# A preamble scheduled by hand and fenced, with two weights converted in it, and weight loads moved to ScalarE's queue

## The chip, the core and the metric

The kernel runs on one core of a Trainium2 chip. Times are microseconds on the device, taken as the median of three runs. Beside them stands one profiled execution with its trace. PE is TensorE (PEld its weight loads), DVE is VectorE, ACT is ScalarE, POOL is GpSimd, and SP is SyncE, which issues transfers and computes nothing.

## The reference

Three stages follow each other. The first is windowed attention over 4 batches, 8 heads, 768 positions and 64 dimensions: each query sees the keys within 16 positions and one summary per block of 32 keys.

```
k_sum = k.reshape(B, H, nb, 32, D).max(axis=3);  v_sum = v.reshape(B, H, nb, 32, D).mean(axis=3)
scores = concat([where(|i - j| < 16, scale * q @ k.T, -1e9), scale * q @ k_sum.T + log(32)])
a = softmax(scores);  x = a @ concat([v, v_sum])            # 3072 tokens x 512
h = x @ w_in;  x = (h * cos(h)) @ w_out                     # 512 -> 2048 -> 512
logits = x @ phi;  d = softmax(logits, over tokens);  slots = d.T @ x      # 8 experts, 4 slots each
out = softmax(logits, over slots) @ (relu(slots @ w1) @ w2)
```

The weights `w_in` and `w_out` arrive as 64-bit numbers, whose two 32-bit halves the kernel turns into one f32 itself.

## The kernel before, in words

The middle stage is the long one. Its tokens are cut into 6 blocks of 512 and the 2048 hidden columns into 16 slices of 128, so that a loop of 96 slots runs block by block over the slices. In slot s PE computes `mm1`, 12 products of 128x512 into `h` (L384, L385, L388), DVE and ACT compute h cos h, and PE multiplies the result by `w_out` two slots later in `mm2`, again 12 products (L425, L426, L429). Every f32 operand is split into a high part that ACT casts (`wih`, `woh`, `gh`, `xh`) and a low part that DVE or POOL subtracts (`wil`, `wol`, `gl`, `xl`), which gives the three products where one would do.

Attention is cut into 24 groups of 4 heads by 4 query blocks. Groups 0 to 3 make the first token block and come in a preamble ahead of the loop. Groups 4 to 23 are worked off between the slots: scores on PE, exponentials on ACT, normalisation, transposes (`tr`, copied to `aT`), and the product with the values (`av`), which is split into `xh` and `xl`.

Each of the 16 weight slices is used by all six blocks and converted once. `load_w` (L119) brings 1 MB `raw` into one of two buffers. `conv_1` reads it twice on ACT (L129 and L130), `conv_2` shifts on DVE (L136), and `conv_3` adds on POOL (L141). Before, the string `PRE` (L44) lists the preamble token by token. It holds the conversions of slices 0 to 3 (`c0` to `c3`), and slice f from 4 on is converted in slot f - 4, whose load is for slice f + 2. The preamble's scores (`first_A`, L236) add the mask on PE, by two products with a split mask (L252), and the exponentials (`first_exps`, L261) read PSUM. The sums of the values, `vs`, are copied by ACT into the last rows of the value tiles (L225).

All instructions before slot 17 are put in an order by a scheduler that simulates the program; from slot 17 on (`MAN0`) PE and SP keep the order of the code. Each engine runs its instructions in order, and SP issues all transfers in one order too. `HB` (L53) sets in half slots where groups 4, 5 and 6, 7 begin; a negative value begins at slot 0. `fill` (L565) issues products of ones with ones that nothing reads.

Of the kernel before, what the change touches and what calls it, by code (L numbers as in the profile page):

```python
# [52 lines left out]
HB = (-4, 14)  # L53
# [25 lines left out]
def body(ctx: ExitStack, tc: tile.TileContext, q0, qk, kT, vn, vx, w, phi, ex, cst, out):  # L79
# [16 lines left out]
    NM = 6 * KC  # L96
    mask = att.tile([128, 6, KC], F32, name="mask", tag="mask", bufs=1)
# [18 lines left out]
    def load_w(f):  # L116
        pool, tag, n = (xres, "xl", 2) if f == 2 else (m2, ("x2", "x2T")[(f - (f > 2)) % 2], 1)
# [3 lines left out]
    def conv_1(f):  # L121

        W[f] = wres.tile([128, 2, 512], F32, name=f"w{f}", tag=f"w{f}")
        pool, tag = (wres, "w15") if f % 2 and f < 15 else (att, "cv")
# [1 line left out]
        nc.scalar.activation(W[f], raw[f][:, :, :, 1].bitcast(F32), AF.Prelu, scale=2.0 ** -111, alpha=-2.0 ** 32)  # L129
# [106 lines left out]
    def first_A(g, j):  # L236

        d = grp[g]
        ps = d["ps", j] = bank(f"sc{g}_{j}")
        c = (g // 2) % 3  # L240
        heads = [slice(64 * hh, 64 * hh + 64) for hh in range(2)]
        p = 2 * (g % 2) + j
        for u in range(4):
            o = QB * (4 * (g // 2) + u)
            for r in heads:
                nc.tensor.matmul(ps[r, u * KC:u * KC + KL], d["q"][r, j, u, :], kfirst[p][r, o:o + KL],
                                 start=u == 0, stop=False)
            for r in heads:
                nc.tensor.matmul(ps[r, u * KC + KL:(u + 1) * KC], d["q"][r, j, u, :], ksums[p][r, :],
                                 start=False, stop=False)  # L250
        for m in (mask_hi, mask_lo):
            nc.tensor.matmul(ps[:, 0:4 * KC], ident8, m[:, c:c + 4, :].rearrange("p w c -> p (w c)"),  # L252
                             start=False, stop=m is mask_lo)
        if j == 0:
            d["mx"] = stat.tile([128, 8], F32, name=f"mx{g}", tag="mx")
        m = d["mx"][:, 4 * j:4 * j + 4]
        nc.vector.tensor_reduce(out=m, in_=ps[:, 0:4 * KC].rearrange("p (w c) -> p w c", c=KC), axis=AX.X,
                                op=ALU.max, negate=True)
        nc.vector.tensor_single_scalar(out=m, in_=m, scalar=SCALE, op=ALU.mult)

    def first_exps(g, j):  # L261
        d = grp[g]
        if j == 0:
            if g % 2 == 0:
                grp["S", g // 2] = att.tile([128, 16, KC], F32, name=f"S{g}", tag="S")
            d["S"] = grp["S", g // 2][:, 8 * (g % 2):8 * (g % 2) + 8, :]
            d["sm"] = stat.tile([128, 8], F32, name=f"sm{g}", tag="sm")
        for u in range(4 * j, 4 * j + 4):
            c = (u % 4) * KC
            nc.scalar.activation(d["S"][:, u, :], d["ps", j][:, c:c + KC], AF.Exp, bias=d["mx"][:, u:u + 1],  # L270
                                 scale=SCALE, accum_out=d["sm"][:, u:u + 1])

    def att_A(g):
# [6 lines left out]
        pss = [ps_m.tile([128, 512], F32, name=f"sc{g}_{hh}", tag="m") for hh in range(2)]  # L280
        for n in range(4):
            for u in (2 * (n % 2), 2 * (n % 2) + 1):
                for hh in range(2):
                    t = d["qk"][64 * hh:64 * hh + 64, n // 2, u, :]
                    o = 64 * (u % 2)
                    nc.tensor.matmul(pss[hh][o:o + 64, n * KC:(n + 1) * KC], t[:, 0:QB], t[:, QB:], start=True, stop=True)  # L286
# [45 lines left out]
    def att_C(g, j):  # L332
# [9 lines left out]
        nc.scalar.copy(aT, ps[:KC, :])  # L342
        d["aT", j] = aT

    def att_D(g):
        d = grp[g]
        ps = bank(f"av{g}") if g < 4 else ps_m.tile([128, 512], F32, name=f"av{g}", tag="m")
        for j in range(2):
            for u in range(4):
                c = 256 * j + QB * u  # L350
                for hh in range(2):
                    r = slice(64 * hh, 64 * hh + 64)
                    a = d["aT", j][:, 128 * u + 64 * hh:] if g < 4 else d["aT", hh][:, 256 * j + 64 * u:]
                    nc.tensor.matmul(ps[r, c:c + QB], d["v"][:KC, j, u, r], a[:, 0:QB], start=True, stop=True)  # L354
# [207 lines left out]

# [12 lines left out]
    def masks():
        nc.vector.tensor_single_scalar(out=ident8, in_=ident, scalar=8.0, op=ALU.mult)
        nc.scalar.copy(mask_hi, mask)
        nc.gpsimd.tensor_tensor(out=mask_lo, in0=mask, in1=mask_hi, op=ALU.subtract)

    def load_mask2(_):  # L580

        nonlocal mask2
        mask2 = att.tile([128, 6, KC], F32, name="mask2", tag="mask", bufs=1)
        nc.sync.dma_start(out=mask2[:, 0:4, :].rearrange("p w c -> p (w c)"), in_=cst[:, NM + 468:NM + 468 + 4 * KC])

    mask2 = None

    C = lambda t, o, n: (lambda _: nc.sync.dma_start(out=t, in_=cst[:, o:o + n]))
    todo = dict(F=lambda _: fill(F0), f=lambda _: fill(NFILL), I=C(ident, NM, 128), M=C(mask.rearrange("p w c -> p (w c)"), 0, NM),
                A=C(avg, NM + 128, 52), S=C(sel, NM + 180, 288), N=load_mask2, P=lambda _: nc.sync.dma_start(out=phis.rearrange("p k s -> p (k s)"), in_=phi),  # L590
                K=load_kraw, Q=load_q_first, W=load_w, B=lambda i: load_vb(0, i), V=load_v, G=load_qk, X=load_vs,
                m=lambda _: masks(), k=ksum, s=scores, e=exps, v=lambda _: vsum_first(), t=turn, d=att_D, c=convert, c1=conv_1,
                w=lambda f: split_w(f, 0), a=att_K)
    for token in PRE.split():
        n = token.lstrip("FfIMNASPKQWBVGXmksevtdcwa")
        todo[token[:len(token) - len(n)]](int(n or 0))
# [347 lines left out]
```

## Time and profile before

| | us |
|---|---|
| median of 3 runs | 783.22 (782.16 to 784.07) |
| profiled execution | 780.9 |
| its span, first to last instruction | 778.9 |
| PE busy in the span | 740.2 (95%) |
| DVE, ACT, POOL busy | 473.6, 433.4, 428.6 |

The profiled execution is 2.3 us below the median, and 2.0 us of it lie outside the span. PE is the busy engine over the whole, but the shares differ by stretch: `fill` products count as busy, and in the first 120 us PE waits at several places. The granted TensorE clock is given as a share of 2.4 GHz; over the span it is 0.987.

### The profile page before, as it was taken

The numbers are of one execution on the slowest core, as the hardware profiler recorded it, in microseconds if no ns is written. First come the engines' busy times: TensorE is split into PE (matmuls) and PEld (weight loads), VectorE is DVE, ScalarE is ACT, GpSimd is POOL, SyncE is SP. The second block draws the span as 40 slices with busy tenths as digits, with TensorE's granted clock in tenths as the row PEclk, the third lists the DMA queues.
The fourth block names the chain that finished last, engine by engine and source line by source line (L and its number), as shares of the span: only waits on it lengthen the run. The fifth ranks groups of instructions, "written<-read, shape, count | busy, mean of one in ns | idle before, by whom it ended". The sixth has DMA issues, their size and how long they took to land.

```text
span 778.9 us, 13853 instructions
## 1 busy us (share of the span) xinstructions
PE 740.2 (95%) x5517; PEld 573.5 (74%) x5517; DVE 473.6 (61%) x686; ACT 433.4 (56%) x786; POOL 428.6 (55%) x302
## 2 busy tenths in 40 slices
PE   9977799998999999998999999999999999999994
PEld 7866678776877787776787777778768888786453
DVE  4578896767477576576575684774773444433523
ACT  4979868636465455574465555464554455443222
POOL 2555884365557657556566566665576665752000
PEclk9997999999999999999999999999999999999998
DMA  9988753121120331311211211301101922328978
GB/s 331 396 264 331 271 164 113 42 97 59 48 95 1 100 105 29 121 68 41 87 44 33 72 40 33 111 0 35 33 1 56 392 93 82 109 81 299 371 306 268
DMA packets 35585, 101.69 MB, mean 131 GB/s; under 512 B 3393, under 2 KB 13889, under 8 KB 33473
## 3 DMA queue, kind: packets, MB, share of 16 engines
q1 hardware_dynamic: 35520, 100.81, 36.8%
q8 instruction: 43, 0.70, 0.4%
q14 instruction: 22, 0.17, 0.1%
HBM read 92.54 MB, written 6.29 MB: 127 GB/s over the span
## 4 chain that ended last, share of the span: by engine, by line
PE 63%; DVE 13%; ACT 12%; DMA 6%; issue 4%; SPq 0%; ACTq 0%; DVEq 0%
PE acc L425 8%; PE h L384 8%; PE acc L426 8%; PE h L385 8%; PE acc L429 7%; PE h L388 7%; PE av L354 3%; DVE S L329 2%; DMA qk<-in_qk_dram 2%; PE yp L842 2%; DMA kr<-in_kT_dram 2%; PE sc L286 2%; PE hp L809 2%; ACT a L404 2%; DVE a L403 2%
## 5 line engine op out<-in xcount | busy, mean ns | idle before, releaser
L373 POOL TENSOR_TENSOR wol<-w,woh 128x512 fp32r<-128x512 f32 x96 | 143.9, 1500 | 115.0 <-ACT woh L372 115.0
L413 POOL TENSOR_TENSOR gl<-a,gh 128x512 fp32r<-128x512 f32 x96 | 129.0, 1343 | 83.8 <-ACT gh L412 78.3
L384 PE MATMUL h<-xh,wih 128*128 128x512 f32 x384 | 156.4, 407 | 6.7 <-DVE a L409 6.6
L425 PE MATMUL acc<-woh,gh 128*128 128x512 f32 x384 | 157.4, 410 | 3.5 <-DVE x L448 3.5
L385 PE MATMUL h<-xl,wih 128*128 128x512 f32 x384 | 152.2, 396 | 0.0
L426 PE MATMUL acc<-wol,gh 128*128 128x512 f32 x384 | 152.1, 397 | 0.0
L373 POOL TENSOR_TENSOR wil<-w,wih 128x512 fp32r<-128x512 f32 x81 | 113.9, 1406 | 42.8 <-PE h L388 24.2
L402 DVE TENSOR_SCALAR a<-h 128x512 f32<-128x512 f32 x96 | 65.9, 686 | 115.8 <-PE h L388 110.7
L404 ACT ACTIVATE a<-a,halfpi 128x512 f32<-128x512 f32 x96 | 69.4, 724 | 115.7 <-DVE a L403 115.4
L388 PE MATMUL h<-xh,wil 128*128 128x512 f32 x384 | 104.9, 395 | 0.0
L429 PE MATMUL acc<-woh,gl 128*128 128x512 f32 x384 | 104.6, 393 | 0.0
L409 DVE TENSOR_TENSOR a<-h,a 128x512 f32<-128x512 f32 x96 | 66.1, 689 | 57.0 <-ACT a L404 56.9
L425 PEld LDWEIGHTS acc<-woh,gh 128*128 128x128 f32 x384 | 72.4, 188 | 28.6 <-issue 11.8
L384 PEld LDWEIGHTS h<-xh,wih 128*128 128x128 f32 x384 | 72.7, 189 | 24.6 <-DVE a L409 8.4
L372 ACT CAST wih<-w 128x512 fp32r<-128x512 f32 x96 | 59.2, 617 | 47.2 <-PE h L385 46.4
L388 PEld LDWEIGHTS h<-xh,wil 128*128 128x128 f32 x384 | 72.5, 189 | 16.3 <-issue 0.2
L429 PEld LDWEIGHTS acc<-woh,gl 128*128 128x128 f32 x384 | 72.1, 189 | 16.4 <-issue 0.6
L385 PEld LDWEIGHTS h<-xl,wih 128*128 128x128 f32 x384 | 72.8, 190 | 15.2 <-issue 0.3
L426 PEld LDWEIGHTS acc<-wol,gh 128*128 128x128 f32 x384 | 72.6, 189 | 14.6 <-issue 0.6
L412 ACT CAST gh<-a 128x512 fp32r<-128x512 f32 x96 | 59.3, 619 | 32.8 <-DVE a L409 32.8
L372 ACT CAST woh<-w 128x512 fp32r<-128x512 f32 x96 | 59.1, 616 | 21.7 <-PE acc L429 20.8
L403 DVE SCALAR_TENSOR_TENSOR a<-a,h 128x512 f32<-128x512 f32 x96 | 65.5, 683 | 2.1
(137 smaller groups left out, 945.8 us busy)
## 6 DMA issues: line engine op xcount, KB each, us to landing
ex<-in_ex_dram SPq DMA_DIRECT2D x64, 512.0 KB
raw<-in_w_dram SPq DMA_DIRECT2D x16, 1024.0 KB
qk<-in_qk_dram SPq DMA_DIRECT2D x20, 736.0 KB
v<-in_vx_dram SPq DMA_DIRECT2D x24, 512.0 KB
kr<-in_kT_dram SPq DMA_DIRECT2D x16, 384.0 KB
vb<-in_vn_dram SPq DMA_DIRECT2D x12, 512.0 KB
out_dram<-o SPq DMA_DIRECT2D x12, 512.0 KB
v<-vs SPq DMA_DIRECT2D x40, 48.0 KB
```

The source lines that it names most:

```text
L372: nc.scalar.copy(hi, W[f][:, part, :])
L373: (eng or nc.gpsimd).tensor_tensor(out=lo, in0=W[f][:, part, :], in1=hi, op=ALU.subtract)
L384: nc.tensor.matmul(h, hi[:, c], xh[s // NF][:, t, :], start=t == 0, stop=False)
L385: nc.tensor.matmul(h, hi[:, c], xl[s // NF][:, t, :], start=False, stop=False)
L388: nc.tensor.matmul(h, lo[:, c], xh[s // NF][:, t, :], start=False, stop=t == 3)
L403: nc.vector.scalar_tensor_tensor(out=a, in0=a, scalar=MAGIC, in1=h, op0=ALU.subtract, op1=ALU.subtract)
L404: nc.scalar.activation(a, a, AF.Sin, bias=halfpi, scale=-TWO_PI)
L409: nc.vector.tensor_tensor(out=a, in0=h, in1=a, op=ALU.mult)
L413: nc.gpsimd.tensor_tensor(out=gl, in0=a, in1=gh, op=ALU.subtract)
L425: nc.tensor.matmul(acc[t], gh[:, c], hi, start=f == 0, stop=False)
L426: nc.tensor.matmul(acc[t], gh[:, c], lo, start=False, stop=False)
L429: nc.tensor.matmul(acc[t], gl[:, c], hi, start=False, stop=f == NF - 1)
```

## The change

The preamble is written out in one order for all five engines, inside a block in which the scheduler keeps that order. Its groups use the same `att_A`, `att_max` and `att_exps` as the later groups: the mask is added by DVE as it moves the scores from PSUM, and the two mask products, the split of the mask and the second mask tile go away. Inside the fence stand the conversions of slices 0 and 1. Those of slices 2 and 3 follow right behind it, issued after the last instructions of the fenced block. DVE in place of ACT copies the transposes of groups 0, 1 and 2. The sums are copied into the value tiles by DVE for groups 0 and 2 and by four transfers for groups 1 and 3. Loads of slices 4 and 5 and of all later ones are issued from ACT's queue, directly behind the conversion that they follow in the code. `HB` becomes (1, 15). The fills are 44 products rather than 70.

```diff
-HB = (-4, 14)
+HB = (1, 15)
-    def load_w(f):
+    def load_w(f, eng=None):
...
-        nc.sync.dma_start(out=raw[f].rearrange("p a c t -> p (a c t)"), in_=w[f].bitcast(I32))
+        return (eng or nc.sync).dma_start(out=raw[f].rearrange("p a c t -> p (a c t)"), in_=w[f].bitcast(I32))
...
     def load_vs(g):
         p = 2 * (g % 2)
-        if g < 4:
-            vs = vsums[0][KL:KC, p:p + 2, :]
-            nc.scalar.copy(grp[g]["v"][KL:KC], vs.unsqueeze(2).to_broadcast([NSUM, 2, 4, 128]))
-            return
...
+    def copy_vs(g):
+        p = 2 * (g % 2)
+        vs = vsums[0][KL:KC, p:p + 2, :]
+        nc.vector.tensor_copy(grp[g]["v"][KL:KC], vs.unsqueeze(2).to_broadcast([NSUM, 2, 4, 128]))
+
+    def turn(g, eng=None):
+        for j in range(2):
+            att_C(g, j, eng or nc.vector)
+
+    with tc.manual_schedule(engines={EE.PE, EE.Activation, EE.DVE, EE.Pool, EE.SP}):
+        load_kraw(0)
+        load_q_first(0)
+        load_kraw(1)
+        load_c(mask.rearrange("p w c -> p (w c)"), 0, NM)
+        load_q_first(2)
...
+        fill(14)
+        ksum(0)
+        ksum(1)
+        scores(0)
+        att_exps(0)
...
+        vsum_first()
+        load_w(2)
+        load_w(3)
+        for g in (1, 3):
+            load_vs(g)
+        lasts = [load_qk(4)]
+        att_exps(3)
+        att_norm(1, nc.gpsimd)
+        copy_vs(0)
+        fill(8)
+        turn(0)
+        fill(6)
+        conv_1(0)
+        load_w(4, nc.scalar)
+        conv_1(1)
+        lasts.append(load_w(5, nc.scalar))
+        turn(2)
+        att_norm(3, nc.gpsimd)
+        copy_vs(2)
+        fill(6)
+        turn(1)
+        conv_2(0)
+        conv_3(0)
+        conv_2(1)
+        lasts.append(conv_3(1))
+        att_D(0)
+        fill(4)
+        turn(3, nc.scalar)
+        att_D(2)
+        split_w(0, 0, nc.vector)
+        att_D(1)
+        lasts += att_D(3)
+
+    for ins in lasts:
+        ctx.enter_context(tc.issue_after(ins.ins))
+    for f in (2, 3):
         conv_1(f)
         conv_2(f)
         conv_3(f)
...
-    for f in range(NPRE, NF):
+    for f in range(4, NF):
...
-            at(c, CP, load_w, f + 2)
+            at(c, CP, load_w, f + 2, nc.scalar)
```

The order shows where the work of the two halves of the change goes. First POOL at the end of the preamble; `S` are attention weights being normalised, `w` and `cv` the halves of a converted slice, `wil` and `wol` low parts of weights. Before:

```order
L329 TENSOR_TENSOR S2_259<-S2_259,rs2_421 128x960
L373 TENSOR_TENSOR wil0_590<-w0_561,wih0_589 128x512
L373 TENSOR_TENSOR wol0_790<-w0_561,woh0_789 128x512
L329 TENSOR_TENSOR S0_206<-S0_206,rs1_469 128x960
L141 TENSOR_TENSOR w1_575<-w1_575,cv1_576 128x1024
L329 TENSOR_TENSOR S2_259<-S2_259,rs3_506 128x960
L141 TENSOR_TENSOR w2_583<-w2_583,cv2_584 128x1024
L373 TENSOR_TENSOR wol1_850<-w1_575,woh1_849 128x512
L141 TENSOR_TENSOR w3_593<-w3_593,cv3_594 128x1024
```

The same place on POOL in the changed kernel:

```order
L295 TENSOR_TENSOR S0_161<-S0_161,rs1_410 128x960
L295 TENSOR_TENSOR S2_215<-S2_215,rs3_469 128x960
L139 TENSOR_TENSOR w0_442<-w0_442,cv0_444 128x1024
L139 TENSOR_TENSOR w1_448<-w1_448,cv1_450 128x1024
L139 TENSOR_TENSOR w2_598<-w2_598,cv2_600 128x1024
L139 TENSOR_TENSOR w3_604<-w3_604,cv3_606 128x1024
L338 TENSOR_TENSOR wol0_713<-w0_442,woh0_712 128x512
L338 TENSOR_TENSOR wol1_757<-w1_448,woh1_756 128x512
```

All conversions now come behind the last normalisation, and the low parts of the first two `w_out` slices behind the conversion of slice 3. Next the end of the preamble on ACT before, from the third group's exponentials on; `aT` are transposed weights, `xh` the high part of the tokens:

```order
L270 ACTIVATE S2_259,sm3_438<-sc3_1_399,mx3_396 128x120 x4
L362 CAST xh0_464<-av0_447 128x2x256
L129 ACTIVATE w2_583<-raw2_154 128x1024
L342 COPY aT1_0_477<-tr1_0_472 120x512
L130 ACTIVATE cv2_584<-raw2_154 128x1024
L342 COPY aT1_1_484<-tr1_1_479 120x512
L234 COPY qk4_567<-ks0_159 128x4x24
L234 COPY qk4_567<-ks1_161 128x4x24
L372 CAST wih1_688<-w1_575 128x512
L372 CAST woh1_849<-w1_575 128x512
L362 CAST xh0_464<-av2_486 128x2x256
```

And in the changed kernel:

```order
L114 DMA raw4_446<-in_w_dram 128x2048
L124 ACTIVATE w1_448<-raw1_137 128x1024
L128 ACTIVATE cv1_450<-raw1_137 128x1024
L114 DMA raw5_452<-in_w_dram 128x2048
L328 CAST xh0_514<-av0_497 128x2x256
L308 COPY aT3_0_527<-tr3_0_522 120x512
L308 COPY aT3_1_534<-tr3_1_529 120x512
L328 CAST xh0_514<-av2_536 128x2x256
L337 CAST wih0_555<-w0_442 128x512
L328 CAST xh0_514<-av1_559 128x2x256
L328 CAST xh0_514<-av3_578 128x2x256
L124 ACTIVATE w2_598<-raw2_390 128x1024
```

Two conversions, six copies and the split of slice 1 have left the stretch ahead of the last `xh`, and two loads have come into it. Last, ACT in the loop of the changed kernel, where before such loads stood on SP between loads of `kr`, `vb`, `v` and `qk`:

```order
L337 CAST wih5_925<-w5_724 128x512
L114 DMA raw9_873<-in_w_dram 128x2048
L124 ACTIVATE w8_947<-raw8_781 128x1024
L128 ACTIVATE cv8_949<-raw8_781 128x1024
L377 CAST gh2_784<-a2_760 128x512
L114 DMA raw10_953<-in_w_dram 128x2048
L124 ACTIVATE w9_1015<-raw9_873 128x1024
L128 ACTIVATE cv9_1017<-raw9_873 128x1024
L114 DMA raw11_1021<-in_w_dram 128x2048
```

A load stands on ACT behind the conversion that frees its buffer, and slice 9 is converted three computing instructions after its own load.

## Rows read from the trace of the kernel before

**Rows 1.** Engines by stretch: busy us, granted clock, DMA share, GB/s.

```profile
0.00:46.46 46.46, 44.64 (x621) 39.34 (x621) 24.40 (x46) 35.13 (x98) 22.72 (x20) 1.00 0.89 330
46.46:90.00 43.54, 30.68 (x231) 23.06 (x228) 35.52 (x44) 38.20 (x77) 24.83 (x13) 0.88 0.85 303
90.00:121.02 31.02, 31.02 (x190) 23.94 (x190) 27.63 (x30) 21.38 (x39) 25.96 (x15) 0.95 0.61 214
```

**Rows 2.** Waits of PE, 46 to 121 us: total, times, longest.

```profile
PE sc L286 <- ACT qk L234: 6.7, 1, 6.7
PE tr L336 <- DVE vs L195: 2.9, 1, 2.9
```

**Rows 3.** PE in order of time: start, us, instruction.

```profile
46.46 0.50 PE L384 MATMUL h<-xh,wih 128*128 128x512 f32 x1
...
110.44 1.04 PE L286 MATMUL sc<-qk 64*64 64x120 f32 x16
...
118.26 0.40 PE L425 MATMUL acc<-woh,gh 128*128 128x512 f32 x1
...
120.11 1.07 PE L429 MATMUL acc<-woh,gl 128*128 128x512 f32 x4
...
121.02 0.40 PE L384 MATMUL h<-xh,wih 128*128 128x512 f32 x1
```

**Rows 4.** Groups by line and shape, 0 to 60 us: busy, mean ns, idle before.

```profile
L141 POOL TENSOR_TENSOR w<-w,cv 128x1024 int32<-128x1024 int32 x7 | 16.6, 2367 | 16.8 <-DVE mx L259 5.8 <-ACT wih L372 4.5 <-DVE w L136 3.6
L270 ACT ACTIVATE S<-sc,mx 128x120 f32<-128x120 f32 x32 | 11.1, 375 | 1.1 <-DVE mx L259 1.1
...
L129 ACT ACTIVATE w<-raw 128x1024 f32<-128x1024 f32 x7 | 8.3, 1186 | 9.0 <-DMA raw<-in_w_dram 9.0
...
L225 ACT COPY v<-vs 24x1024 f32<-24x1024 f32 x4 | 4.1, 1042 | 0.5 <-DVE vs L204 0.5
...
L363 DVE TENSOR_TENSOR xl<-av,xh 128x512 fp32r<-128x512 f32 x4 | 2.8, 688 | 1.7 <-ACT xh L362 1.7
...
L290 DVE SCALAR_TENSOR_TENSOR S<-sc,mask 128x480 f32<-128x480 f32 x2 | 1.2, 652 | 0.5 <-PE sc L286 0.5
L298 DVE TENSOR_REDUCE mx<-S 128x8 f32<-128x960 f32 x1 | 1.1, 1144 | 0.0
```

**Rows 5.** Keys and first exponentials in order of time.

```profile
8.72 0.95 DVE L170 TENSOR_REDUCE ks<-kr 128x24 f32<-128x768 f32 x1 [3.36 <-DMA kr<-in_kT_dram]
...
13.95 0.36 ACT L270 ACTIVATE S<-sc,mx 128x120 f32<-128x120 f32 x1
```

**Rows 6.** DVE and POOL side by side, in order of time.

```profile
28.75 1.79 POOL L329 TENSOR_TENSOR S<-S,rs 128x960 f32<-128x960 f32 x1 [3.40 <-DVE rs L328]
...
29.17 1.92 DVE L136 TENSOR_SCALAR w<-w 128x1024 int32<-128x1024 int32 x1
...
46.90 0.68 DVE L136 TENSOR_SCALAR w<-w 128x1024 int32<-128x1024 int32 x1
...
75.12 1.16 DVE L329 TENSOR_TENSOR S<-S,rs 128x960 f32<-128x960 f32 x1
76.20 0.68 DVE L373 TENSOR_TENSOR wil<-w,wih 128x512 fp32r<-128x512 f32 x1
```

**Rows 7.** POOL, conversions and low parts, in order of time.

```profile
44.34 2.38 POOL L141 TENSOR_TENSOR w<-w,cv 128x1024 int32<-128x1024 int32 x1 [0.70 <-DVE w L136]
...
113.03 1.74 POOL L413 TENSOR_TENSOR gl<-a,gh 128x512 fp32r<-128x512 f32 x1
116.97 1.30 POOL L413 TENSOR_TENSOR gl<-a,gh 128x512 fp32r<-128x512 f32 x1 [2.21 <-ACT gh L412]
```

**Rows 8.** One weight load on SP, and the conversion that waits for it.

```profile
43.97 0.33 SPq L119 DMA_DIRECT2D raw<-in_w_dram  x1
...
51.92 1.12 ACT L129 ACTIVATE w<-raw 128x1024 f32<-128x1024 f32 x1 [3.90 <-DMA raw<-in_w_dram]
```

**Rows 9.** SP's waits over the whole span: total, times, longest.

```profile
SPq L119 <- ACT cv L130: 27.0, 12, 5.2
```

More of the change, by code (lines that the diff above doesn't have):

```diff
@@ L93, in body @@
     att = att_cm.__enter__()
-    NM = 6 * KC
-    mask = att.tile([128, 6, KC], F32, name="mask", tag="mask", bufs=1)
+    NM = 4 * KC
+    mask = att.tile([128, 4, KC], F32, name="mask", tag="mask", bufs=1)
     ident = const.tile([128, 128], F32, name="ident")
@@ L212, in load_qk @@
         t = att.tile([128, 2, 4, QB + KC], F32, name=f"qk{g}", tag="qk")
-        nc.sync.dma_start(out=t.rearrange("p j w c -> p (j w c)"), in_=qk[g - 4])
+        issue = nc.sync.dma_start(out=t.rearrange("p j w c -> p (j w c)"), in_=qk[g - 4])
         grp[g] = dict(qk=t)
+        return issue
     def load_v(g):
@@ L234, in att_K @@
             nc.scalar.copy(grp[g]["qk"][:, j, :, QB + KL:], ks.unsqueeze(1).to_broadcast([128, 4, NSUM]))
[L236 to L271, printed above, removed]
     def att_A(g):
@@ L279, in att_A @@
         d["S"] = grp["S", g // 2][:, 8 * (g % 2):8 * (g % 2) + 8, :]
-        pss = [ps_m.tile([128, 512], F32, name=f"sc{g}_{hh}", tag="m") for hh in range(2)]
+        pss = [bank(f"sc{g}_{hh}") if g < 4 else ps_m.tile([128, 512], F32, name=f"sc{g}_{hh}", tag="m") for hh in range(2)]
         for n in range(4):
[L282 to L286, printed above, removed]
+            j, us, c = n // 2, (2 * (n % 2), 2 * (n % 2) + 1), n * KC
+            tiles = [(u, hh, slice(64 * hh, 64 * hh + 64), slice(64 * (u % 2), 64 * (u % 2) + 64)) for u in us for hh in range(2)]
+            if g < 4:
+                w, p = QB * (4 * (g // 2)), 2 * (g % 2) + j
+                for u, hh, r, o in tiles:
+                    nc.tensor.matmul(pss[hh][o, c:c + KL], d["q"][r, j, u, :], kfirst[p][r, w + QB * u:w + QB * u + KL],
+                                     start=True, stop=True)
+                for u, hh, r, o in tiles:
+                    nc.tensor.matmul(pss[hh][o, c + KL:c + KC], d["q"][r, j, u, :], ksums[p][r, :], start=True, stop=True)
+            else:
+                for u, hh, r, o in tiles:
+                    t = d["qk"][r, j, u, :]
+                    nc.tensor.matmul(pss[hh][o, c:c + KC], t[:, 0:QB], t[:, QB:], start=True, stop=True)
         c = (g // 2) % 3
-        m = mask2[:, c:c + 2, :].rearrange("p w c -> p (w c)").unsqueeze(1).to_broadcast([128, 2, 2 * KC])
+        m = mask[:, c:c + 2, :].rearrange("p w c -> p (w c)").unsqueeze(1).to_broadcast([128, 2, 2 * KC])
         for hh in range(2):
@@ L352, in att_D @@
                     r = slice(64 * hh, 64 * hh + 64)
[L353 to L354 removed]
+                    product = nc.tensor.matmul(ps[r, c:c + QB], d["v"][:KC, j, u, r],
+                                               d["aT", hh][:, 256 * j + QB * u:256 * j + QB * u + QB], start=True, stop=True)
         b, o = g // 4, 256 * ((g // 2) % 2)
@@ L361, in att_D @@
         hi, lo = (x[b][:, p:p + 2, o:o + 256] for x in (xh, xl))
-        nc.scalar.copy(hi, ps)
-        nc.vector.tensor_tensor(out=lo, in0=ps, in1=hi, op=ALU.subtract)
+        return product, nc.scalar.copy(hi, ps), nc.vector.tensor_tensor(out=lo, in0=ps, in1=hi, op=ALU.subtract)
     wi, wo = {}, {}
@@ L568, in fill, with load_c, scores @@
             nc.tensor.matmul(warmth[:, 0:128], ones, ones, start=True, stop=True)
-    def convert(f):
+    def load_c(t, o, n):
+        nc.sync.dma_start(out=t, in_=cst[:, o:o + n])
+    def scores(g):
+        att_A(g)
+        att_max(g, True)
+    def copy_vs(g):
[11 more added lines that the diff above has]
+        load_q_first(2)
+        load_kraw(2)
+        load_q_first(1)
+        load_kraw(3)
+        load_q_first(3)
+        load_c(ident, NM, 128)
+        load_c(avg, NM + 128, 52)
+        for i in range(3):
+            load_vb(0, i)
+        load_w(0)
+        for g in (0, 2):
+            load_v(g)
+        load_w(1)
+        for g in (1, 3):
+            load_v(g)
+        fill(14)
[3 more added lines that the diff above has]
+        att_exps(0)
+        fill(2)
+        ksum(2)
+        ksum(3)
+        scores(2)
+        att_exps(2)
+        fill(4)
+        att_norm(0, nc.gpsimd)
+        scores(1)
+        att_exps(1)
+        att_norm(2, nc.gpsimd)
+        scores(3)
+        vsum_first()
+        load_w(2)
+        load_w(3)
+        for g in (1, 3):
+            load_vs(g)
[20 more added lines that the diff above has]
+        att_D(0)
+        fill(4)
+        turn(3, nc.scalar)
[6 more added lines that the diff above has]
+    for f in (2, 3):
         conv_1(f)
@@ L573, in convert @@
         conv_3(f)
[L575 to L596, printed above, removed]
+    load_qk(5)
+    att_K(4)
+    att_K(5)
+    load_v(4)
+    load_v(5)
+    load_c(sel, NM + 180, 288)
+    nc.sync.dma_start(out=phis.rearrange("p k s -> p (k s)"), in_=phi)
+    load_vs(4)
+    load_vs(5)
     for g in range(4, 24):
```

41 lines of the change are left out of this document (14 added, 27 removed).

## The prediction, made before the change was run

> **What bounds the kernel now.** I read the busy shares by stretch first, then PE's waits, then PE in order of time. The reader is to see that the loop is PE's, but not at its start. Up to the loop's first product at 46.46 PE shows 44.64 us busy, but much of that is fill and small products; that stretch is a chain through key loads, DVE, ACT and POOL [rows 1, 3]. From 46.46 to 90 PE is busy 30.68 of 43.54 us at a mean granted clock of 0.88, while ACT is busy 38.20. From 90 to 121 PE is never idle, and the clock is 0.95 [rows 1]. PE's two longest waits between 46 and 121 us are 6.7 and 2.9 us, one for a copy on ACT and one for DVE [rows 2]. So the change, which touches only what stands ahead of slot 17, can win at two places: the preamble's 46.46 us, and behind it 12.9 us of idle time and up to 7 us of low clock (means of 0.88 over 43.54 us and 0.95 over 31.02 are 10.4 and 3.1 us at half of 2.4 GHz).
>
> I measure both at one state: the end of `mm2` of slot 6, at 121.02 us [rows 3]. By then `mm1` of slots 0 to 9 and `mm2` of 0 to 6 are done, and groups 4 and 5 are through. Behind it the two kernels have the same work, which PE sets.
>
> **The preamble.** The exponentials of the first group began at 13.95 us. Ahead of them came the maximum of the second key tile, which waited for its load until 8.72, and on ACT the split of the mask and a conversion, 0.8 and 2.1 us [rows 5, 4]. Now the second key tile is the third load, not the fifth, with 1.0 MB and not 1.4 up to its end. I put it at 6.5 us, between 5.5 and the old 8.7. Then come 0.95 (block maximum), 0.1 of products, two masked copies of 0.65 and one row maximum of 1.14 [rows 4, 5]: first exponentials at about 10. Four groups of eight at 0.375 are 12.0 on ACT [rows 4]. The fourth key tile, now the eighth load, makes ACT wait some 2 us ahead of the second group: 24.0. Slices 0 and 1 follow there, four instructions of 1.19, of which 0.13 overlaps: 28.2. The shift and POOL's two additions of 2.37, behind the last normalisation, end at 35.1, in which 0.7 is lost between DVE and POOL. The last `xl` is ready near 37, and the first `mm1` ends near 39.
>
> ACT's four copies of sums, 1.04 each, go [rows 4]. No row shows their replacements on DVE: two copies of 24x1024, between the 0.68 of the shift alone and 1.04, say 1.0 each; six copies of transposes at about the 0.69 of `xl`, whose source lies in PSUM too [rows 4, 6]. These 6.1 us stand on DVE, which has about 26 us of work between 4.4 and 37, so they fit; uncovered they would cost all of that. The transfers for groups 1 and 3 are issued at about 22 us behind 2 MB of weights, which at 330 GB/s [rows 1] take 6.4 us; they are needed at 31. Late by that whole burst they would cost up to 2 us. The two mask products are on PE, which waits there anyway: nothing.
>
> At the edges 35.1 could be 31.8 (no wait at all) or 39.1 (keys as late as before).
>
> **The loop's start.** Here I look at POOL and DVE together. The shift of a slice took 0.68 us alone, but 1.92 beside a normalisation of 1.79 on POOL, and it ended 0.55 us after POOL did; a low part on POOL took 1.30 alone and 1.74 right behind other work [rows 6, 7]. So I count as one queue the POOL operations and those of DVE that only touch SBUF. The Trainium skill, "SBUF — State Buffer", section "SBUF: two separate sides", calls the port that both share an exclusive lock held for the whole instruction; the 1.92 agrees. By that rule alone the sum below would end at 98.3, with no gap between the instructions.
>
> From the end of the addition for slice 3 at 46.72 to the end of the low part `gl` of slot 6 at 114.77 are 68.05 us [rows 7]. In them lie 12 conversions (2.37 + 0.68), 12 low parts on POOL (1.30), 8 `wil` (0.68) and 2 normalisations (1.16): 59.9 us, a share of 0.88 [rows 4, 6, 7].
>
> In the changed kernel, from 35.1 to the same `gl`, the queue holds slices 2 to 13 (12 conversions, 36.6), 14 low parts (18.2), 9 `wil` (6.1) and 2 normalisations (2.3): 63.2 us. Two conversions moved from ahead of the fence into the loop, and the last two come later than this `gl`. At a share of 0.88 that is 71.8, so `gl` ends at 106.9 and `mm2` of slot 6 at 107.9, with the last four products behind it [rows 3].
>
> ACT is the check. Up to `gh` of slot 6 it has 13 conversions (27.3), 17 weight casts, 7 sines and 7 casts, 16 exponentials, 5 table loads, the small copies, and ten load issues at the 0.33 to 0.43 that one takes on SP, 4 us: some 66 us from 28.2, so 94 without waits. Walking its order, with 4.9 us from a load's issue to its use, adds 10, since some slices are converted two or three instructions after their load: 104 to 105. It is second, close behind.
>
> The Trainium skill, "DMA: Bandwidth & Descriptors", section "Issuing engines are not separate DMA queues", says that transfers of all engines run on the same 16 DMA engines and that another issuing engine only saves issue time. By that the move to ACT's queue brings nothing, and costs ACT's time. SP stood 27.0 us in front of such loads, in 12 waits, with other loads behind [rows 9]; that ends, but I count no gain for it, since before, too, ACT waited 3.9 us for the one shown, and did not wait for most others [rows 8, 4].
>
> **The sum.** At 107.9 the changed PE still has to do, to reach the old state, `mm1` of slot 9 (2.8), half of the scores of group 6 (0.5) and the value products of group 5 (1.0): 4.3 us. 121.0 - 107.9 - 4.3 = 8.8. Slices 14 and 15 then put 6.1 us more on POOL and DVE in slots where PE would otherwise be alone; I take 1 off, between 0 and 2. The gain is 7.8. Moving `HB` shifts groups 4 and 6 by a few slots; their work is the same, and group 7 ends one `mm2` (2.8 us) ahead of slot 16, which covers its casts. The profiled execution of 780.9 would be 773.1. The median is 2.3 above it, so 775.4.
>
> With the edges (31.8 and a share of 0.95; 39.1 and 0.80) `mm2` of slot 6 ends at 99.2 or 119.0: a gain of 17.5, or a loss of 2.3, and 4.3 with the 2 us of the last slices. That is 765.7 to 787.5.
>
> **The rivals.**
>
> Given back: the earlier start is spent in the queue of conversions. For it speaks that the queue was already at 0.88 in a stretch where ACT waited for loads, so that compressing it lengthens more waits; against it, that those waits are among what goes. At a share of 0.80 `mm2` of slot 6 ends at 115.0, and the gain falls to 0.7: 782.5. Up to 4 us of gain I count here.
>
> Slower: ACT's queue stalls on its own loads. An issue stands behind a conversion, and slices 8, 9, 12 and 13 are wanted within 3 to 5 us of it. A load issued at 43.97 could be used only at 51.92, 7.95 us later [rows 8]. If that is what loads take here, ACT waits some 14 us more than in the walk, `gh` of slot 6 comes at about 118.5, `mm2` ends near 120.5, and the sum turns to a loss of 4.8: 788. It decides from about 6.3 us between issue and use. Against it: that load stood in a saturated stretch (DMA share 0.85), and fewer loads stand around later (0.61) [rows 1].
>
> Larger: the shared queue is no limit and ACT is. With half its waits `mm2` of slot 6 ends at 100 to 101, a gain of 14.7 to 15.7: 768. For it speaks that POOL sat idle 16.8 us before its conversions in the first 60 us [rows 4]; against it the 1.92 us beside the 0.68.
>
> **How the numbers follow.** The forecast (gains of 4 to 12 us) gets 0.58, given back 0.18, slower 0.12, larger 0.12. Within 0.2%, 1.6 us, a measurement of this kernel can't tell from no change. Of given back 0.10 falls there and 0.08 is faster. So faster 0.58 + 0.12 + 0.08 = 0.78, same 0.10, slower 0.12. The range for 8 in 10 leaves out most of slower and the far edge of larger: 768.5 to 783.5.
>
> **What would show it.** The first loop product starts near 33 to 35 us, its first `mm1` ends near 39. First exponentials near 10, the second addition on POOL ends near 35. PE waits more, not less, in the first 60 us of the loop, mostly for `wih`, `wil` and `gh`, and at a granted clock below 1. `mm2` of slot 6 ends near 108. Behind it the traces run alike. I am wrong in the preamble if that addition ends past 39, and wrong in the queue if POOL and DVE together show a share far from 0.88; wrong on ACT's queue if waits for `raw` there exceed 15 us.

## The result, and the profile after

The changed kernel takes 792.92 us (median; 791.88 to 795.4), the kernel before 782.69 in the same session: ratio 1.0141, 95% interval 1.0102 to 1.0181. 775.4 was forecast, within 768.5 to 783.5; the time lies outside that range. In the profiled execution (795.4 us, the longest of the four) the span is 793.7 us at a mean granted clock of 0.971, against 778.9 and 0.987. So the two profiles lie 14.5 us apart (795.4 against 780.9) where the medians lie 10.2 apart, and what is read from the profiles below adds up to the larger figure.

PE has the same loop work in both, so I compare them by work left: to each moment of the kernel before belongs the moment at which the other kernel has as much product time still to do (every product at its spacing at 2.4 GHz, fill left out). The table has the difference of the two moments, in us, negative where the other leads, from one profiled execution each. The rows below the first are runs that are told in the next section:

```
at us of before      46     58     94    118    148    190    687
changed kernel     -8.1   +0.4   -5.5   -3.1   +4.8  +10.5  +14.4
e1 HB undone      -10.6   -6.7   -3.2   +0.5   +0.1    0.0   +2.9
e4 both undone    -11.5   -5.3   -4.3   -3.5   +0.4   +0.1   +2.4
e6 e4, 2+3 fenced -10.4   -9.3   -6.6   -6.3   -3.3   -3.3   -2.1
e7 all fenced      -8.9   -8.2   -8.0   -7.7   -4.3   -4.6   -2.4
f2 e7, HB -4,12   -10.4   -8.6   -8.5   -8.4   -2.5   -6.9   -5.2
f3 before, -4,12   -0.4   -2.0   -2.1   -2.5   -2.6   -7.0   -5.9
g1 after, -4,12    -8.7   -4.5   -0.4   +0.5   +6.8   +2.5   +5.0
```

So the preamble's 8 us were there, were given back in the first 20 us of the loop, came back in part between 60 and 94 us (there the kernel before waits 1.82 us near 64 and 1.36 and 2.94 us between 84 and 89) and were lost in two steps behind 130 us: 8 us by 148, 6 more by 190. Some 4 us trickle away later. Between 36 and 700 us PE is idle for 37.5 us (25.0 before). At 1.2 GHz a product takes twice as long (0.80 us below, against 0.40 in [rows 3]), so half of PE's busy time at that clock is lost: 13.9 us (5.1 before). Together that is 21.3 us more, and less the lead of 7.5 at the first product it is 13.8.

Engines by stretch, the changed kernel (columns as in [rows 1]):

```profile
0.00:38.92 38.92, 29.94 (x552) 26.83 (x552) 24.70 (x45) 21.13 (x76) 13.20 (x14) 0.95 0.97 350
38.92:90.00 51.08, 37.08 (x213) 27.64 (x213) 41.12 (x48) 42.41 (x81) 30.43 (x16) 0.84 0.72 265
90.00:121.02 31.02, 28.31 (x214) 21.65 (x214) 27.62 (x32) 24.24 (x35) 26.92 (x14) 1.00 0.63 227
121.02:160.00 38.98, 35.31 (x216) 28.07 (x211) 25.05 (x35) 26.55 (x65) 15.58 (x12) 0.91 0.22 68
160.00:210.00 50.00, 44.12 (x293) 34.21 (x293) 29.21 (x39) 23.58 (x38) 22.88 (x18) 0.93 0.20 66
```

and the last two stretches in the kernel before, at full clock:

```profile
121.02:160.00 38.98, 38.90 (x256) 31.21 (x255) 27.76 (x39) 26.18 (x61) 18.13 (x13) 1.00 0.22 69
160.00:210.00 50.00, 47.04 (x332) 36.51 (x331) 28.30 (x42) 26.49 (x42) 27.31 (x21) 1.00 0.19 62
```

PE's longest waits in the changed kernel from its first loop product to 215 us (compare [rows 2]):

```profile
PE h L349 <- DVE a L374: 16.2, 5, 5.9
PE h L353 <- DVE wil L338: 7.3, 1, 7.3
PE sc L252 <- DVE xl L328: 1.3, 1, 1.3
```

**The preamble and what stands behind it**, in order of time:

```profile
10.63 0.40 ACT L285 ACTIVATE S<-S,mx 128x120 f32<-128x120 f32 x1 [8.41 <-DVE mx L264]
...
29.41 0.38 ACTq L114 DMA_DIRECT2D raw<-in_w_dram  x1
29.84 1.16 ACT L124 ACTIVATE w<-raw 128x1024 f32<-128x1024 f32 x1 [3.89 <-DMA v<-vs]
...
34.98 0.33 ACTq L114 DMA_DIRECT2D raw<-in_w_dram  x1
35.41 0.59 ACT L328 CAST xh<-av 128x512 fp32r<-128x512 f32 x1 [3.38 <-DMA v<-vs]
...
39.51 1.16 ACT L124 ACTIVATE w<-raw 128x1024 f32<-128x1024 f32 x1
```

```profile
25.68 3.58 SPq L224 DMA_DIRECT2D v<-vs  x4
```

```profile
32.18 2.34 POOL L139 TENSOR_TENSOR w<-w,cv 128x1024 int32<-128x1024 int32 x1 [0.70 <-DVE w L134]
45.44 2.41 POOL L139 TENSOR_TENSOR w<-w,cv 128x1024 int32<-128x1024 int32 x1 [10.93 <-DVE w L134]
...
110.58 1.29 POOL L378 TENSOR_TENSOR gl<-a,gh 128x512 fp32r<-128x512 f32 x1
...
118.37 2.84 POOL L139 TENSOR_TENSOR w<-w,cv 128x1024 int32<-128x1024 int32 x1
```

```profile
34.58 1.69 PE L319 MATMUL av<-aT,v 120*64 120x64 f32 x32 [3.95 <-DMA v<-vs]
...
38.92 0.80 PE L349 MATMUL h<-xh,wih 128*128 128x512 f32 x1
...
54.32 2.08 PE L353 MATMUL h<-xh,wil 128*128 128x512 f32 x4 [7.31 <-DVE wil L338]
...
114.59 1.19 PE L394 MATMUL acc<-woh,gl 128*128 128x512 f32 x4
```

POOL stands still for 10.93 us between slices 1 and 2, since ACT takes up slice 2 at 39.51, behind the last `xh`. The last addition of the loop ends at 121.2 (113.1 before, where the `gl` of [rows 7] follows it): PE starts 7.5 us earlier, the conversions run later than before from slice 2 on.

**The loss at 140 us.** ACT and PE in order of time:

```profile
136.43 0.40 ACT L285 ACTIVATE S<-S,mx 128x120 f32<-128x120 f32 x1 [3.03 <-DVE mx L264]
...
138.82 1.28 ACT L369 ACT_TABLE_LOAD   x1
140.12 0.72 ACT L369 ACTIVATE a<-a,halfpi 128x512 f32<-128x512 f32 x1
```

```profile
136.31 0.67 DVE L368 SCALAR_TENSOR_TENSOR a<-a,h 128x512 f32<-128x512 f32 x1
```

```profile
141.62 0.80 PE L349 MATMUL h<-xh,wih 128*128 128x512 f32 x1 [3.67 <-DVE a L374]
```

The sine could have run at 137.0. It stands behind exponentials of group 7, for whose maximum ACT waits 3.03 us, and behind the table load. PE waits 3.67 us for `mm1` of slot 12 and then runs below full clock (0.66 from 140 to 150).

**The loss at 187 us.** PE and ACT:

```profile
179.15 1.04 PE L252 MATMUL sc<-qk 64*64 64x120 f32 x16
...
193.01 0.79 PE L349 MATMUL h<-xh,wih 128*128 128x512 f32 x1 [5.88 <-DVE a L374]
```

```profile
185.36 0.45 ACT L229 COPY qk<-ks 128x96 f32<-128x96 f32 x2 [1.17 <-DMA qk<-in_qk_dram]
...
187.11 1.80 ACT L273 ACTIVATE S<-S 128x1920 f32<-128x1920 f32 x1
188.93 1.28 ACT L369 ACT_TABLE_LOAD   x1
190.23 1.33 ACT L369 ACTIVATE a<-a,halfpi 128x512 f32<-128x512 f32 x2
```

The exponential of groups 8 and 9 needs the second scores of group 9, which PE reaches only at 179.15; a copy just ahead of it on ACT also waits 1.17 us for its load. The sines for slots 16 and 17 stand behind it on ACT, and `mm1` of slot 18 waits for them.

### The profile page after: what moved, and what is told of

Same layout as the page of the kernel before. It is cut to its first block, busy times and chain, and to the rows that moved or that the text cites. A ratio compares the mean times of both kernels' runs of the same rounds, so it can differ in the third digit from the quotient of the medians.

```text
span 793.7 us, 13712 instructions
## 1 busy us (share of the span) xinstructions
PE 735.2 (93%) x5449; PEld 567.5 (72%) x5449; DVE 481.0 (61%) x690; ACT 429.7 (54%) x777; POOL 425.3 (54%) x300
## 4 chain that ended last, share of the span: by engine, by line
PE 61%; DVE 14%; DMA 10%; ACT 9%; issue 4%; SPq 0%; ACTq 0%; DVEq 0%
PE h L349 8%; PE acc L390 8%; PE h L350 8%; PE acc L391 7%; PE h L353 7%; PE acc L394 7%; DMA qk<-in_qk_dram 5%; PE av L319 3%; DMA kr<-in_kT_dram 2%; DVE S L295 2%; PE yp L868 2%; PE sc L252 2%; PE hp L835 2%; ACT a L369 2%; DVE a L368 2%
## 5 line engine op out<-in xcount | busy, mean ns | idle before, releaser
L349 PE MATMUL h<-xh,wih 128*128 128x512 f32 x384 | 159.3, 415 | 19.9 <-DVE a L374 19.7
L350 PE MATMUL h<-xl,wih 128*128 128x512 f32 x384 | 154.7, 403 | 0.0
L338 POOL TENSOR_TENSOR wil<-w,wih 128x512 fp32r<-128x512 f32 x80 | 110.9, 1387 | 48.8 <-PE h L353 28.0
L353 PE MATMUL h<-xh,wil 128*128 128x512 f32 x384 | 107.6, 403 | 7.3 <-DVE wil L338 7.3
L350 PEld LDWEIGHTS h<-xl,wih 128*128 128x128 f32 x384 | 74.4, 194 | 15.4 <-issue 0.5
```

Of the source, the lines that this page charges most:

```text
L338: (eng or nc.gpsimd).tensor_tensor(out=lo, in0=W[f][:, part, :], in1=hi, op=ALU.subtract)
L349: nc.tensor.matmul(h, hi[:, c], xh[s // NF][:, t, :], start=t == 0, stop=False)
L350: nc.tensor.matmul(h, hi[:, c], xl[s // NF][:, t, :], start=False, stop=False)
L353: nc.tensor.matmul(h, lo[:, c], xh[s // NF][:, t, :], start=False, stop=t == 3)
```

## The experiments

All of three rounds; ratios are to the kernel before in the same session.

**HB and the queue of the loads, each undone.**

```
e1, on the changed kernel   -HB = (1, 15)
                            +HB = (-4, 14)
e2, on the changed kernel   -load_w(4, nc.scalar)        (5 alike)
                            +load_w(4)
                            -at(c, CP, load_w, f + 2, nc.scalar)
                            +at(c, CP, load_w, f + 2)
e3, on the kernel before    -HB = (-4, 14)
                            +HB = (1, 15)
e4: the edits of e1 and e2 together
```

> The changed kernel with HB back at (-4, 14), nothing else undone. At equal remaining work of PE the changed kernel led by 7 to 8 us between 98 and 122 us, then fell back by 6.7 us at 140 to 146, by 5.5 at 182 to 188 and by some 6 later. Theory A (the later start half-slots of groups 4 to 7 push their exponentials between the loop's activations): the falls at 140 and 185 go, 771 to 781 us. Theory B (the raw loads on ACT's queue): HB is harmless, the two falls stay, 790 to 795 us. Theory C (every kernel gets its own order of DVE and ACT from the planner, which does not see what this chip will do, and any change deals it anew): falls of 3 to 7 us somewhere else, 783 to 792 us.

> The changed kernel with all raw weight loads (4 and 5 in the preamble, and those of the loop) issued from SP again, HB left at (1, 15). Theory A: the falls at 140 and 185 stay, 789 to 797 us. Theory B: ACT's waits and issue time go, 775 to 785 us. Theory C: the order is dealt anew, falls of a few us elsewhere, 785 to 797 us.

> The kernel before with HB at (1, 15) and nothing else. Theory A: the same falls as in the changed kernel, 12 us or more, without the 8 us of the preamble: 792 to 804 us. Theory B: within 2 us of the kernel before, 780 to 785 us. Theory C: 783 to 795 us, with falls at other places.

> The changed kernel with both undone: HB at (-4, 14) and the raw loads on SP; what is left is the preamble by hand. Theory A: 771 to 781 us, as with HB alone undone. Theory B: 772 to 783 us, as with the loads alone undone. Theory C: 780 to 792 us.

e1: 784.71, ratio 1.0050 (1.0032 to 1.0067). e2: 791.92, 1.0134 (1.0114 to 1.0153). e3: 790.65, 1.0115 (1.0095 to 1.0136). e4: 782.93, 1.0018 (1.0005 to 1.0031). HB costs the kernel before 9.3 us, e4's kernel 9.0 (e2 against e4), the changed kernel 0.9%, some 7. Theory A has the places of the two losses: PE's waits from 121 to 215 us are, in e1,

```profile
PE tr L302 <- DVE S L295: 1.6, 1, 1.6
PE h L349 <- DVE a L374: 1.3, 1, 1.3
```

and in e3, where HB alone is changed,

```profile
PE h L384 <- DVE a L409: 6.5, 2, 5.2
PE acc L425 <- ACT gh L412: 1.5, 1, 1.5
```

But A's size is wrong: with HB undone 771 to 781 was expected, and e3 came out below its range too; only e2 lies in it. From 142 us on e1 and e4 run level with the kernel before; their lead of 11 us was gone. (By the table the changed kernel's lead between 94 and 118 us, given in the expectation as 7 to 8, is 3 to 5.)

Theory C, that any change deals the scheduler's orders anew, has all four times in its ranges. e3 fell at the same two places, as A said, and by some 5 us between 100 and 110 us too. But of the two falls only the second, at slot 18, goes with HB in every pair. At slot 12 PE waits no more than 1.3 us in e2, with the new HB,

```profile
PE h L349 <- DVE a L374: 7.2, 2, 5.9
```

and e4, with the old one, still loses 3.9 us between 118 and 148. So the first loss is HB's in the changed kernel (against e1) and in the kernel before (e3), and not with the loads on SP.

The loads on ACT's queue cost 1.8 us (e1 against e4) or nothing that can be told (the changed kernel against e2): theory B falls.

**Where the preamble's lead goes.** On e4:

```
e5: key tiles of the second batch loaded and summed in slots 3 to 6
    (slot 0 in e4), its value tiles in slots 0 to 3
e6: +conv_1(2), conv_2(2), conv_3(2) in the fence behind conv_3(1)
    +conv_1(3), conv_2(3), conv_3(3) at its end
    -for f in (2, 3): ... behind it
e7: both, and +split_w(1, 0, nc.vector) in the fence
```

> Built on the preamble by hand alone (HB at (-4, 14), raw loads on SP; 782.9 us, where PE waits 10.2 us for the low part wil of slot 1, which stands on DVE behind a key sum whose tile is still being loaded). Here the four key tiles of the second batch are loaded and summed in slots 3 to 6, and its value tiles in slots 0 to 3. Theory K (the preamble's lead goes in DVE and SP waiting in order for these key tiles): the wait for wil falls below 4 us and the time to 775 to 779 us. Theory Q (it goes in the queue of conversions, with POOL idle some 11 us ahead of the third slice): PE waits a few us later instead, 781 to 784 us. Theory P (the planner's order loses whatever is gained, at another place each time): 780 to 786 us, with a new wait past 100 us.

> Built on the preamble by hand alone (782.9 us). Here slices 2 and 3 are converted inside the fence: ACT's two instructions for slice 2 go where it stands idle from 32 to 35 us, those for slice 3 behind the last xh. Theory Q: POOL's addition for slice 2 ends near 37 us and not near 48, 777 to 780 us. Theory K: the wait for wil of slot 1 stays at 7 to 10 us, 781 to 784 us. Theory P: 780 to 786 us.

> Both of these, and the split of the second weight slice (wih, wil of slot 1) inside the fence too. Theories K and Q: no wait over 4 us in the first three slots, and both gains together, 770 to 777 us. Theory P: 779 to 786 us.

e5: 781.85, 1.0024 (1.0010 to 1.0039). e6: 778.66, 0.9984 (0.9970 to 0.9997). e7: 779.05, 0.9991 (0.9979 to 1.0004). Each mends its place. The wait for `wil`, 10.2 us in e4, falls to 0.8 in e5,

```profile
53.20 2.07 PE L353 MATMUL h<-xh,wil 128*128 128x512 f32 x4 [10.16 <-DVE wil L338]
```

```profile
46.01 1.19 PE L353 MATMUL h<-xh,wil 128*128 128x512 f32 x4 [0.83 <-DVE wil L338]
```

in e6 POOL runs slices 0 to 2 in one go,

```profile
29.72 7.82 POOL L139 TENSOR_TENSOR w<-w,cv 128x1024 int32<-128x1024 int32 x3 [0.69 <-DVE w L134]
```

and in e7 the low part of slot 6 ends at 106.1 us:

```profile
104.39 1.75 POOL L378 TENSOR_TENSOR gl<-a,gh 128x512 fp32r<-128x512 f32 x1
```

The leads at 118 us are 8.2, 6.3 and 7.7 us, and at 148 us 3.3, 3.3 and 4.3. So K and Q are right about the places. In time e6 fell in Q's range, 777 to 780, and gained 0.34% on e4, 2.7 us (their intervals are separate). K's 775 to 779 for e5 and the 770 to 777 of both for e7 did not come; there P's ranges held (the scheduler, which the expectations call planner, loses elsewhere what is gained).

**What sets the loss at slot 18.**

```
e8: HB = (1, 14)    e10: MAN0 = 15    e11: HB = (-4, 15)   on the changed kernel
e9: v(3) in the buffer w6, load_qk(5) in the fence, on e6
e12: MAN0 = 15 on e9
```

> The changed kernel with HB at (1, 14): the second number back (groups 6 and 7, by one half-slot), the first not (groups 4 and 5, by five). HB as a whole costs the changed kernel 8.2 us (792.9 against 784.7). Theory A1 (the one half-slot of groups 6 and 7 puts their exponentials ahead of the activation at 140 us): 784 to 787 us, no wait over 2 us between 135 and 150. Theory A2 (the five half-slots of groups 4 and 5 make everything behind them late): 790 to 795 us.

> The changed kernel with PE and SP taken by hand from slot 15, not 17; HB stays at (1, 15). In the changed kernel's own order the second scores of group 9 stand behind mm1 of slot 16 (its first six products) and all of mm2 of slot 14, in the kernel before ahead of both for the most part; here they stand ahead of both again. Theory S (scores that come late on PE delay the exponential, and the exponential stands on ACT ahead of the sine that slot 18 waits for): the wait of 5.9 us at 187 to 193 us falls under 2.5, and the time by 4 to 8, 785 to 789 us. Theory A2 (only the groups' start half-slots count): the wait stays, 791 to 795 us.

> The changed kernel with HB at (-4, 15): groups 4 and 5 at their old half-slots, 6 and 7 at their new. With (1, 15) it took 792.9 us, with (1, 14) 787.8, with (-4, 14) 784.7. If the two numbers act by themselves, 789 to 791 us. If the second acts only through the order of the scores at slot 16 (Theory S), it depends on whether that order comes out bad here: 784 to 786 us with a wait under 2.5 us at slot 18, 788 to 792 with one of 4 to 6.

> Built on e6_conv_in_fence (778.7 us), where ACT still stands some 5 us in front of the copy into the query and key tile of group 5, whose load waits for the buffer of the value tile of group 3. Here that value tile lies in the unused buffer of weight slice 6 and the load of group 5 is issued in the fence, right behind that of group 4. Theory K (queues that wait in order in the first three slots give the lead back): ACT's wait for qk and PE's for the scores (4.5 us) go, 773 to 777 us. Theory P (the planner's orders lose it again behind slot 7): PE leads by 8 us or more at 120 us and the time is still 777 to 781 us.

> e9_early_qk5 with PE and SP by hand from slot 15. Theory S: 1 to 5 us faster than e9, according to how much PE waits at slots 15 to 18 there. Theory P: within 1.5 us of e9.

e8: 787.83, 1.0108 (1.0093 to 1.0123). e10: 788.09, 1.0080 (1.0052 to 1.0109). e11: 792.61, 1.0165 (1.0142 to 1.0187). e9: 785.24, 1.0070 (1.0046 to 1.0093). e12: 786.70, 1.0078 (1.0053 to 1.0104). e10's waits from 121 to 215 us:

```profile
PE h L349 <- DVE a L374: 3.7, 2, 1.9
PE sc L252 <- DVE xl L328: 1.1, 1, 1.1
```

Of the 5.9 us 1.8 are left (the 1.9 in this line is at slot 12), with PE's order ahead of slot 15 as it was. Theory S said that; the time is 4.8 us lower (the two kernels ran in different sessions, and the ends of their intervals just overlap). Here are all kernels by the number of loop products (those of `mm1` and `mm2`) that PE has ahead of the second scores of group 9, with the gap before slot 18:

```
ahead   gap before slot 18, us
348     none: the six with HB at (-4, 12) or (-4, 13) below
348     1.8 e10, 2.8 e12
369     1.1 to 1.4: before, e1, e4, e6, e7
377     3.0 e9
379     4.2 e5
380     4.5 e8
382     5.0 to 5.9: changed, e2, e3, e11
```

That is the order in which PE was told to work, and it could be counted before any run. Two things limit it. HB is one way to a late place, not the only one: e5 and e9 have the old HB and 379 and 377 products ahead. And the count is not the only thing that delays the exponential: in e10 and e12 it is 348 and a gap is left. There the exponential stands on ACT behind a copy that waits 3.00 and 6.44 us for its load, in e12

```profile
173.97 0.27 ACT L229 COPY qk<-ks 128x96 f32<-128x96 f32 x1 [6.44 <-DMA qk<-in_qk_dram]
```

So e12 was no faster than e9, where S expected 1 to 5 us; it lies within P's 1.5 us. A1 fails: with (1, 14) the loss between 136 and 148 us stays (4.4 us); A2's 790 to 795 did not come either. The two halves of HB do not add: (-4, 15) costs as much as (1, 15). e9 took away PE's wait of 4.5 us for `qk`, and the wait for `a` next to it grew from 5.2 to 7.8, so K fails; P is right that the gain goes elsewhere, but its range, 777 to 781, failed too: e9 is slower than e6.

**Groups 6 and 7 earlier.** HB = (-4, 12) on e6 (f1), e7 (f2), the kernel before (f3), the changed kernel (g1) and e4 (g2); (-4, 13) on e6 (f4).

> e6_conv_in_fence (778.7 us) with HB at (-4, 12): groups 6 and 7 two half-slots earlier than in the kernel before. Theory G (their place caps what a lead is worth): no wait over 1 us at slots 10 to 13, lead behind 148 us 5 us or more instead of 3.3, 773 to 777 us. Theory P (the planner's orders spend any lead): 777 to 784 us.

> e7_fence_wil_keys (779.1 us, the largest lead at 118 us with that of e5: 7.7) with HB at (-4, 12). Theory G: 771 to 776 us, lead behind 148 us 6 us or more. Theory P: 777 to 784 us.

> The kernel before with HB at (-4, 12), without any lead. Theory G: no gain worth the name, since the groups were not what PE waited for there: 778 to 784 us. Theory P: anything, 778 to 790 us. If the earlier half-slot is a gain by itself, whatever the preamble: 774 to 778 us.

> e6_conv_in_fence with HB at (-4, 13), one half-slot earlier than in the kernel before. Theory G: between e6 and f1, 774 to 778 us. Theory P: 777 to 784 us.

> The changed kernel with HB at (-4, 12), everything else as in it, the raw loads on ACT's queue too. Its order on PE from mm2 of slot 7 to slot 18 is that of f2 (774.2 us) and f3 (777.5). Theory R (the order on PE in slots 8 to 18 decides, not the lead at its start): 774 to 779 us, lead over the kernel before near 2 us at 142 us and near 7 at 190, where the changed kernel was 10 behind. Theory L (the lead and the edits of f2 count): 779 to 786 us, since with HB undone the changed kernel was at 784.7.

> e4_old_hb_sp (782.9 us) with HB at (-4, 12). Its order on PE has both transposes of group 6 inside mm1 of slot 11 and those of group 7 split over slots 12 and 13, as f1 (783.3) and f4 (783.8) have theirs bunched. Theory R: 780 to 786 us. Theory L: near f3 or better, 774 to 779 us.

f1: 783.25, 1.0021 (1.0000 to 1.0041). f2: 774.22, 0.9917 (0.9888 to 0.9947). f3: 777.47, 0.9946 (0.9927 to 0.9965). f4: 783.76, 1.0031 (1.0016 to 1.0046). g1: 782.41, 1.0025 (1.0005 to 1.0044). g2: 780.86, 1.0003 (0.9989 to 1.0018). In all six the gap at slot 18 is gone, and from 148 to 190 us each gains some 3 to 5 us on the kernel before. f3's waits from 121 to 215 us are only

```profile
PE acc L425 <- DVE x L448: 0.4, 1, 0.4
```

Before 148 us the theories fail. R: g1 has f3's order on PE and loses 6 us at 120, where PE waits for DVE's masking of group 7's scores,

```profile
PE sc L252 <- DVE S L256: 3.7, 2, 2.9
```

and ends at 782. G holds for f2 only: f1 and f4 lose 10.5 and 8.7 us between 118 and 148, and both are slower than e6, from which they were made. L holds for g1 and fails for g2, where R's range holds. f2 beats both kernels, 6.9 us under the one before; but f3, which has no preamble by hand, has an interval that overlaps f2's, and both lead by the same 7 us at 190 us. So the gain that is shown is that of the one slot (two half-slots) by which groups 6 and 7 come earlier, on the kernel before, on e7 and, against (1, 15), on the changed kernel; on e4 no gain is clear and on e6 there is a loss.

What stays open: why the lead at 118 us shrinks by 148 in every kernel that got one from the preamble by hand (e6 by 3.0, f2 by 5.9), while f3, without that preamble, keeps its 2.5. In that stretch PE waits mostly for `a`, `gh` or scores, at most 3.7 us at a time, each kernel elsewhere. That other engines have no such lead there speaks for them as the bound; no run separates it from the planner's orders.

## Why the prediction was wrong, step by step

**The preamble: right, but for one term.** First exponentials at 10.63 (10 forecast), the last end at 23.9 (24.0), the second addition at 34.5 (35.1). The copies on DVE cost less than set: 0.69 for 24x1024 (1.0), 0.62 for transposes (0.69). Too small was the term for the transfers, "up to 2 us": they were issued at 25.68, not 22, PE waited 3.95 us, and the first loop product came at 38.92, not 33 to 35. Part of this is ACT's, whose load issues at 29.41 and 34.98 held it for 3.89 us ahead of slice 1 and 3.38 ahead of the first `xh`. With the same preamble and the issues on SP the first product is at 35.0 (e4) to 37.1 us (e5), with them on ACT at 36.4 (e1) to 38.9.

**The queue of POOL and DVE: the rule held, its start did not.** I let slice 2 follow slice 1 at once. Behind the fence it came 10.93 us later. From 45.4 us the queue's 63.2 us of work, at the forecast's prices, took 66.5, a share of 0.95, and `gl` of slot 6 ended at 111.9, not 106.9. `mm2` of slot 6 ended at 115.8, not 107.9: its last four products came 3.9 us behind that `gl` and not 1.0, since PE had scores of group 6 ahead of them and waited 1.3 us there. By the forecast's sum 121.0 - 115.8 - 4.3 leaves 0.9 us of the 8.8; by work left the lead at 118 us is 3.1. In e7, where slices 2 and 3 stand in the fence, `gl` ended at 106.1 and the lead at 118 us was 7.7, near the 8.8 (`mm2` of slot 6 itself ended at 114.2, other products having gone first). So the missed term was the ACT half of slices 2 and 3 behind the last `xh`. The Trainium skill, "SBUF — State Buffer", section "SBUF: two separate sides", calls the port pair that DVE and POOL share an exclusive lock; the share of 0.95 and shifts of 2 us and more beside POOL agree.

**"HB harmless": the step that failed.** I held that moving the groups leaves their work the same and that PE sets the time behind slot 6. The work was the same and the order was not: 13 more loop products ahead of the second scores of group 9, exponentials of group 7 ahead of a sine. ACT did not take the sines ahead of them, PE waited 3.67 and 5.88 us, and its granted clock was 1.2 GHz behind each wait. It costs 7 to 9 us, shown by undoing it (e1, e2 against e4) and by doing it alone (e3). What does the harm is the order that the scheduler makes of it, not the number itself: e5 and e9 got gaps of 4.2 and 3.0 us at slot 18 with the old HB.

**"Behind it the traces run alike": wrong too.** Even with the old HB a lead of 8 us at 118 us is one of 2.4 at the end (e7). In the changed kernel 2.9 us go at slot 48, with the same instructions in the same order as before: a copy on ACT waits 2.31 us for its load, not 0.70, the exponential and `x` follow, and PE waits 2.23 us for `x` and not 1.09, with the clock at 1.2 GHz behind it. Why the load took longer is not shown. The changed kernel, then the kernel before:

```profile
410.20 0.45 ACT L229 COPY qk<-ks 128x96 f32<-128x96 f32 x2 [2.31 <-DMA qk<-in_qk_dram]
```

```profile
424.14 0.77 PE L390 MATMUL acc<-woh,gh 128*128 128x512 f32 x1 [2.23 <-DVE x L413]
```

```profile
396.93 0.45 ACT L234 COPY qk<-ks 128x96 f32<-128x96 f32 x2 [0.70 <-DMA qk<-in_qk_dram]
```

```profile
410.87 0.47 PE L425 MATMUL acc<-woh,gh 128*128 128x512 f32 x1 [1.09 <-DVE x L448]
```

**The rivals.** ACT's queue: wrong in the loop, where ACT's waits for `raw` are 1.7 us in all; 15 had been the mark. The Trainium skill, "DMA: Bandwidth & Descriptors", section "Issuing engines are not separate DMA queues", says that another issuing engine only saves issue time. The runs agree in so far as the move gains nothing: it costs 0 to 1.8 us. Given back was right in kind, and its 115.0 for the end of `mm2` of slot 6 is near the 115.8 that came. But it got there by a share of 0.80, where the share was 0.95 from a later start. It had a chance of 0.18 and no loss beyond it, and it gave no weight to orders that the scheduler deals anew.

By size: 17.5 us lie between forecast and result. HB explains 7 to 9, the loads on ACT's queue up to 2 (784.71 against 782.93), slices 2 and 3 behind the fence 2.7 (0.34% between e4 and e6), and the rest, 4 to 8, is lead that no kernel carried to the end.

## What to carry to other kernels

Where each engine has its instructions in one fixed order, a changed start time is a changed order: before calling it harmless, count for each long operation on the second engine (here the exponential, ahead of a sine) how much work now stands ahead of the product that feeds it. A lead of the bounding engine is worth something only if the engines that feed it get the same lead: look whether the last conversion, not the first product, came earlier. And before spending effort on the start, try the one number that places the next stage: one slot was worth 0.5% on the kernel before (f3), where the rewritten preamble with the old number and loads was worth nothing (e4). But try it again on each kernel: on e6 the same slot was a loss.

## What the runs showed of the hardware that was not expected

A load issue on ACT's queue is not free where it has to wait. In the changed kernel ACT stood 3.89 us ahead of slice 1 and 3.38 us ahead of the first `xh`, both put down to the small transfers of means. In all six kernels with these issues on ACT it stood 3.0 to 4.0 us at the first place, and the first `xh` began at 33.1 to 35.4 us. In the four with the same preamble and the issues on SP (e2, e4, e5, g2) there is no wait at the first place, and the first `xh` began at 29.6 to 30.8 us. A wait of PE can cost more than itself: behind the 3.67 us at 141.62 and the 5.88 at 193.01 the first product takes 0.80 and 0.79 us, not the 0.40 of full clock [rows 3], and the granted clock is 0.66 from 140 to 150 us and from 190 to 200. From 135 to 200 us PE is idle for 9.6 us and loses another 5.9 at 1.2 GHz.
